# Weight rounding spread evenly over the first batch's first layer, each piece finished one product later, and factors kept in DRAM one by one

## The chip, the core and the metric

The kernel runs on one core of a Trainium2 chip. The metric is device time in microseconds (us) of one execution. A profiled execution gives a trace: start, length and releaser of every instruction on TensorE (PE; its weight loads are PEld), VectorE (DVE), ScalarE (ACT), GpSimd (POOL) and on SyncE (SP), which here only issues DMAs.

## The reference

A q/k-normalised attention followed by a two-layer MLP with the activation h − tanh(h); batch 8, 12 heads, 448 positions, head size 64, model width 768, hidden width 2048. Inputs are float32, but the two weights arrive as float64.

```python
q_n, k_n = (rmsnorm(q, g_q), rmsnorm(k, g_k))
scores = scale * np.matmul(q_n, k_n.transpose(0, 1, 3, 2))
attn = softmax(scores)
x = np.matmul(attn, v).transpose(0, 2, 1, 3).reshape(B * S, H * D)
h = x @ w_in
out = ((h - np.tanh(h)) @ w_out).astype(np.float32)
```

## The kernel before

**Two streams on one TensorE.** Attention is worked off in 48 slots, one for each batch and pair of heads. The first batch's six slots (`first_slot`) run alone, with nothing of the MLP beside them. From then on (`early_slot`, later `slot`) every slot calls `run(gap)` between its parts, and `run` puts matmuls of the MLP of the batch before into the gaps. The order of all instructions on each engine is that in which the program writes them (a manual schedule): an engine that waits holds all that stands behind it.

**The MLP as seven products.** Layer 1 (`hidden`) cuts both matrices into 2x2 blocks and forms the result from 7 products in place of 8, for each of four `SETS` j of hidden rows. `ORDER = (1, 5, 6, 2, 3, 7, 4)` is the order of the products p; a product is 12 matmuls of 128x128 by 224 columns into one PSUM bank out of three ("mm"). I number the first batch's 28 products 0 to 27 in the order in which they run. Products 2, 3 and 7 add onto the banks of 1, 5 and 6, so TensorE may begin them only when VectorE or ScalarE has read the older content (`use`, lines 826 to 860), and each next product 1, 5, 6, 4 takes a bank that an older `use` must have read: L831, L833, L841, L837/L838, L845 and L812 on VectorE release banks.

**Weights of the first batch.** The float64 weights are rounded to float32 on the chip, in 32 pieces (`PIECES`) of 128x768: 0 to 15 of w_in (four for each set), 16 to 31 of w_out. A piece n goes through five stations:

- load: a DMA of 768 KB into a raw buffer (`weight_load`, L272 for w_in in four DMAs, L276 for w_out). From piece 8 on there are three raw buffers (`w_raw`), so the load of piece n+3 waits until piece n is finished (`place_free`).
- a: two instructions on ScalarE (`round_weight_a`, L71 and L72).
- b: three on VectorE (`round_weight_b`, L78, L79, L82).
- c: one on GpSimd (`round_weight_c`, L90), after which the raw buffer is free.
- when a set's four pieces are finished, four sums of them (`combine_weights`; L335 on VectorE, "combos" below, for products 5, 6, 3, 7).

`weight(to)` takes pieces until `to` are taken: for each it issues a of piece n, then b of piece n−1, then c of piece n−1 (`finish_weights`), then the loads that have become possible. So b and c of a piece come when the next piece is taken. The list `due` says how many pieces are to be taken before each of the 28 products; before the change its steps are uneven, so that pieces 7, 8, 9, 10, 11, 12, 13, 14, 15, 16, 17, 18, 19, 20, 21, 22, 23 are taken at products 0, 1, 3, 5, 7, 9, 11, 13, 15, 18, 19, 21, 22, 23, 25, 26, 27.

**Keeping the factors.** The seven factors of each set are written to DRAM (`keep_weights`, L343, seven DMAs of 384 KB in a row on SP) for the later batches. Sets 0 and 3 use one half of the weight memory (`w_half[0]`), set 1 the other, set 2 the ring; a new piece may overwrite a place only when its factor has been kept.

**Layer 2 of the first batch** (`project_first`, L952) uses the rounded w_out directly, 16 matmuls of 448 columns for each of six row blocks, and takes pieces 24 to 31 meanwhile. Later batches (`project`, and `hidden` with b > 0) read the kept factors through a ring of buffers.

**The attention part of a slot** that matters here, in order: totals (L658) and the reciprocal `rs` of them (L663, VectorE, which releases the "sc" bank into which `turn` then transposes at L432); scores of the next slot (L531, two banks at a time) with exp on ScalarE (L537; `p`, then `p_last` for the last keys, then `p_full`); values (L585, L635); division into `xT` (L719). In the `scores` call after the values TensorE takes a bank that `p_last`'s exp must have read.

Of the kernel before, what the change touches and what calls it, by code (L numbers as in the profile page):

```python
# [67 lines left out]
def round_weight_a(nc, raw, dst):  # L68

    lo, hi = raw[:, :, 0], raw[:, :, 1]  # L70
    nc.scalar.activation(dst, hi.bitcast(F32), AF.Abs, scale=2.0**-16)  # L71
    nc.scalar.mul(lo, lo.bitcast(U32), 2.0**-29)  # L72


def round_weight_b(nc, raw, dst):

    bits = dst.bitcast(I32)
    nc.vector.tensor_scalar(out=dst, in0=dst, scalar1=HI_MIN, scalar2=HI_MAX, op0=ALU.max, op1=ALU.min)  # L78
    nc.vector.tensor_scalar(  # L79
        out=bits, in0=bits, scalar1=4, scalar2=1, op0=ALU.logical_shift_left, op1=ALU.logical_shift_right  # L80
    )
    nc.vector.scalar_tensor_tensor(  # L82
        out=bits, in0=raw[:, :, 1], scalar=-(2**31), in1=bits, op0=ALU.bitwise_and, op1=ALU.bitwise_or
    )


def round_weight_c(nc, raw, dst):

    bits = dst.bitcast(I32)
    nc.gpsimd.tensor_tensor(out=bits, in0=bits, in1=raw[:, :, 0], op=ALU.add)  # L90
# [54 lines left out]
def bounded_path(tc, ctx, q, k, v, moe_w_in, moe_w_out, out, g_col, ident, ones, half_ones, neg_half, early):  # L145
# [17 lines left out]
    nc = tc.nc  # L163
# [5 lines left out]
    CD, CF = DM // P, DFF // P  # L169
# [5 lines left out]
    EARLY, PIECES = 8, 2 * CF  # L175
    HS = S // 2
    HC, HF = CD // 2, CF // 2
    SETS = CF // 4
    ORDER = (1, 5, 6, 2, 3, 7, 4)
# [57 lines left out]
    raws = {}  # L237
# [12 lines left out]
    def weight_piece(n):  # L250

        if n < CF:
            j, blk = n // 4, n % 4
            p, low, i = ((1, 0, 0), (0, 1, 0), (4, 1, 1), (2, 0, 1))[blk]
            return 2 * j + low * HF, i, built(j, p)
        i, t = 1 - (n - CF) // HF, n % HF
        if i == 0:
            t = t // 2 + t % 2 * (HF // 2)
        return 2 * t, i, w_half[i][t]

    def weight_load(n):

        f, i, _ = weight_piece(n)
        if n < EARLY:
            raw = stage[:, n % NSTAGE * 2 * DM : (n % NSTAGE + 1) * 2 * DM]
        else:
            raw = wp.tile([P, 2 * DM], I32, name="w_raw", bufs=3)
        if n < CF:
            rows = w_in_words[i * HALF : (i + 1) * HALF, f * 2 * P : (f + 2) * 2 * P]
            rows = rows.rearrange("(c h m r) f -> m h r c f", c=HC, h=2, m=2)  # L270
            for r in range(4):
                nc.sync.dma_start(  # L272
                    out=raw[r * BL : (r + 1) * BL].rearrange("p (c f) -> p c f", c=HC), in_=rows[r // 2, r % 2]
                )
        else:
            nc.sync.dma_start(  # L276
                out=raw.rearrange("p (f c) -> p f c", f=2),
                in_=w_out_words[f * P : (f + 2) * P, 2 * i * HALF : 2 * (i + 1) * HALF].rearrange(
                    "(f p) c -> p f c", p=P
                ),  # L280
            )
        raws[n] = raw.rearrange("p (n w) -> p n w", w=2)

    def weight_dst(n):
        return weight_piece(n)[2].rearrange("p f n -> p (f n)")

    done = [0, 0, 0]
    kept = [0, 0]
    combos = []

    def place_free(n):

        if n < EARLY:
            return n - NSTAGE < done[2]
        return n - 3 < max(done[2], EARLY)

    def load_weights(to):

        while done[0] < min(to, PIECES) and place_free(done[0]):
            weight_load(done[0])  # L300
            done[0] += 1

    def weight(to):

        while done[1] < min(to, PIECES):
            n = done[1]
            round_weight_a(nc, raws[n], weight_dst(n))
            if n:
                round_weight_b(nc, raws[n - 1], weight_dst(n - 1))
            done[1] = n + 1  # L310
            finish_weights(n)
            load_weights(n + (3 if n < EARLY - 3 else 4))
            if kept[1] < kept[0] and n >= 4 * kept[0] + 2:
                keep_weights()
        if done[1] == PIECES > done[2]:
            round_weight_b(nc, raws[PIECES - 1], weight_dst(PIECES - 1))
            finish_weights(PIECES)

    def finish_weights(to):
        while done[2] < to:  # L320
            round_weight_c(nc, raws.pop(done[2]), weight_dst(done[2]))
            done[2] += 1
            if done[2] % 4 == 0 and done[2] <= CF:
                combine_weights(done[2] // 4 - 1)
            keep_w_out(done[2] - 2)
# [13 lines left out]

    def keep_weights():  # L340
        j = kept[1]
        for p in ORDER:
            nc.sync.dma_start(out=w_in_dram[j, p].rearrange("p (f n) -> p f n", f=2), in_=built(j, p))  # L343
        kept[1] = j + 1

    def combine_w_out(f):

# [391 lines left out]
    late = {}  # L739


    due = [EARLY + (m + 1) // 2 for m in range(8)] + [12]
    due += [12 + m // 2 + 1 for m in range(8)]
    due += [CF + HF * (m + 1) // 11 for m in range(11)]
    assert len(due) == 7 * SETS and due[-1] == CF + HF

    def part(name):
# [5 lines left out]
    def products(b, layer, count, width, depth, moving, done_with):  # L753

        took = 4 * HS / ENGINE_NS
        banks = {}  # L760

        def product(j, p, bank, first):
            if b == 0:
                weight(due[7 * j + ORDER.index(p)])
                combine(1)
                while any(c[:2] == (j, p) for c in combos):
                    combine(1)
                w = built(j, p).rearrange("p f (n d) -> p (f n) d", d=P)
            else:
                ring_load(ring_steps.index((b, layer, j, p)) + 5)  # L770
                step_out()
                w = ring_tiles[b, layer, j, p].rearrange("p (n d) -> p n d", d=P)
            for f in range(width):
                for c in range(depth):
                    nc.tensor.matmul(  # L775
                        bank[:, f * HS : (f + 1) * HS], lhsT=w[:, c * width + f, :], rhs=moving[p](c),
                        start=(first and f == 0 and c == 0), stop=(f == width - 1 and c == depth - 1),
                        skip_group_check=not first,
                    )
                    if f < width - 1 or c < depth - 1:  # L780
                        yield took
            now = late["todo"]
            late["todo"] = []
            for fn in now:
                fn()

        for j in range(count):
            use = done_with(j)
            for p in ORDER:
                first = p not in (2, 3, 7)  # L790
                bank = banks[p] = mm_bank() if first else banks[{2: 1, 3: 5, 7: 6}[p]]
                yield from product(j, p, bank, first)
                use(p, bank)
                yield took
# [128 lines left out]
    def project_first(b):  # L923

        g = late["g"]
        for fn in late["todo"]:
            fn()
        late["todo"] = []
        took = 4 * S / ENGINE_NS
        for m in range(CD * CF):  # L930
            k, f = m // CF, m % CF
            n = (k + HC) % CD
            if f == 0:
                bank = mm_bank()
            if f == CF // 2:
                step_out(2)
            if k < HC:
                weight(CF + HF + HF * (m + 1) // (HC * CF))
            elif m < HC * CF + 2:
                keep_w_out(PIECES - 2 + m - HC * CF)  # L940
            elif (m - HC * CF) % 4 == 0 and m - HC * CF <= 4 * HF:
                for fn in late["keep"]:
                    fn()
                late["keep"] = []
                combine_w_out((m - HC * CF) // 4 - 1)
            elif m == CD * CF - 12:
                ring_load(2)
                for fn in late["keep"]:
                    fn()
            elif m == CD * CF - 10:  # L950
                ring_load(4)
            nc.tensor.matmul(  # L952
                bank[:, :S], lhsT=w_out_row(f, n // HC)[:, n % HC * P : (n % HC + 1) * P], rhs=g[:, f, :],
                start=(f == 0), stop=(f == CF - 1),
            )
            if f == CF - 1:
                y = part("s2").rearrange("p f s -> p (f s)")
                nc.scalar.copy(out=y, in_=bank[:, :S])
                store(b, n, y)
            yield took  # L960
        wp_stack.close()
        late["tg"] = pool("tg", bufs=1)
        late["blocks"] = pool("blocks", bufs=1)
# [511 lines left out]
```

## Time and profile before

| | us |
|---|---|
| median of 3 runs (range) | 1382.25 (1381.95 to 1382.39) |
| the profiled execution | 1382.1 |
| its span from first to last instruction | 1380.2 |
| TensorE busy in the span | 1347.5 |
| VectorE busy | 891.1 |
| ScalarE busy | 551.7 |
| GpSimd busy | 553.7 |
| products of the first batch (L775, first matmul to the first of L952) | 79.47 to 184.39 |

Busy shares of the whole span say little about a stretch of some 100 us that lies ahead of 1,100 us of steady work; the stretch has to be read by its own windows and its own timeline. Lengths in the timeline of TensorE are modelled at the end of each group, so the distance from one group's start to the next group's start is the safer measure.

### The profile page before, as it was taken

The numbers are of one execution on the slowest core, as the hardware profiler recorded it, in microseconds if no ns is written. First come the engines' busy times: TensorE is split into PE (matmuls) and PEld (weight loads), VectorE is DVE, ScalarE is ACT, GpSimd is POOL, SyncE is SP. The second block draws the span as 40 slices with busy tenths as digits, with TensorE's granted clock in tenths as the row PEclk, the third lists the DMA queues.
The fourth block names the chain that finished last, engine by engine and source line by source line (L and its number), as shares of the span: only waits on it lengthen the run. The fifth ranks groups of instructions, "written<-read, shape, count | busy, mean of one in ns | idle before, by whom it ended". The sixth has DMA issues, their size and how long they took to land.

```text
span 1380.2 us, 29907 instructions
## 1 busy us (share of the span) xinstructions
PE 1347.5 (98%) x11840; PEld 1127.5 (82%) x11840; DVE 891.1 (65%) x1378; ACT 551.7 (40%) x1314; POOL 553.7 (40%) x345
## 2 busy tenths in 40 slices
PE   7989899999999999999999999999999999999997
PEld 3467654478998998899899889989988998999997
DVE  4999889856854776567765568547765677533311
ACT  7856555244433443334433344334433344211100
POOL 4656566224632356215542346323563155302300
PEclk9999999999999999999999999999999999999999
DMA  7789788965676567567657656765665665556664
GB/s 169 180 226 238 242 255 225 256 166 145 184 199 160 153 189 195 155 145 203 186 147 200 169 147 190 197 156 154 192 190 157 155 196 168 141 162 183 192 187 90
DMA packets 367656, 249.90 MB, mean 181 GB/s; under 512 B 281748, under 2 KB 309780, under 8 KB 367508
## 3 DMA queue, kind: packets, MB, share of 16 engines
q1 hardware_dynamic: 367504, 247.90, 66.7%
q8 instruction: 96, 1.57, 0.5%
q14 instruction: 52, 0.43, 0.1%
q10 hardware_dynamic: 4, 0.00, 0.0%
HBM read 214.40 MB, written 33.42 MB: 180 GB/s over the span
## 4 chain that ended last, share of the span: by engine, by line
PE 89%; DVE 5%; DMA 2%; SPq 2%; ACT 1%; issue 1%; POOL 0%; ACTq 0%; DVEq 0%
PE mm L775 67%; PE sc L531 8%; PE sc L597 6%; PE mm L952 5%; PE sc L585 1%; PE sc L635 1%; DVE w_out L335 1%; DVE rs L663 1%; DMA gT<-in_moe_w_in_dram 1%; DMA w_raw<-in_moe_w_in_dram 1%; DVE w_out L82 1%; SPq L125 1%; DMA w_in<-w_out 1%; DVE xT L719 0%; PE mm L635 0%
## 5 line engine op out<-in xcount | busy, mean ns | idle before, releaser
L775 PE MATMUL mm<-xT,w_f 128*128 128x224 f32 x1392 | 275.6, 354 | 0.0
L775 PEld LDWEIGHTS mm<-xT,w_f 128*128 128x128 f32 x1392 | 262.1, 190 | 10.2 <-issue 10.2
L775 PEld LDWEIGHTS mm<-gT,w_f 128*128 128x128 f32 x1344 | 252.8, 190 | 12.8 <-issue 8.4
L775 PE MATMUL mm<-gT,w_f 128*128 128x224 f32 x1344 | 263.0, 354 | 0.0
L812 POOL TENSOR_TENSOR gT<-s,th 128x448 f32<-128x448 f32 x96 | 119.9, 1256 | 329.2 <-ACT th L811 323.0
L531 PE MATMUL sc<-qT,kT 64*32 64x448 f32 (+1 forms) x3072 | 215.5, 501 | 9.3 <-ACT p_last L537 8.4
L488 POOL TENSOR_TENSOR rr_mine<-rr_mine,neg_half 128x28 f32<-128x28 f32 x33 | 158.1, 4791 | 147.6 <-DVE rr_mine L486 105.4
L775 PE MATMUL mm<-tt,w_f 128*128 128x224 f32 x1044 | 208.6, 353 | 0.0
L775 PEld LDWEIGHTS mm<-tt,w_f 128*128 128x128 f32 x1044 | 197.0, 190 | 4.4 <-issue 4.4
L775 PE MATMUL mm<-tg,w_f 128*128 128x224 f32 x1008 | 197.5, 352 | 0.0
L775 PEld LDWEIGHTS mm<-tg,w_f 128*128 128x128 f32 x1008 | 190.7, 190 | 0.0
L531 PEld LDWEIGHTS sc<-qT,kT 64*32 64x32 f32 x3072 | 70.6, 106 | 78.1 <-issue 55.1
L712 DVE TENSOR_TENSOR xT<-xT,sc 128x448 f32<-128x448 f32 x35 | 21.7, 621 | 138.6 <-PE sc L531 94.9
L597 PE MATMUL sc<-p,v_nat 64*32 64x448 f32 x1120 | 110.5, 536 | 0.0
L734 POOL TENSOR_TENSOR tt<-xT,tt 128x224 f32<-128x224 f32 x23 | 31.2, 1356 | 166.9 <-DVE xT L716 147.2
L537 ACT ACTIVATE p<-sc 128x448 f32<-128x448 f32 x132 | 71.7, 543 | 48.2 <-PE sc L531 36.3
L811 ACT ACTIVATE th<-s 128x448 f32<-128x448 f32 x96 | 54.5, 573 | 69.6 <-DVE s L841 30.2
L687 ACT COPY sum_g<-sum 32x14 f32<-32x14 f32 x280 | 56.3, 201 | 55.4 <-DVE sum L679 44.1
L952 PE MATMUL mm<-gT,w_out 128*128 128x448 f32 x192 | 74.6, 543 | 0.3 <-POOL w_out L90 0.3
L952 PEld LDWEIGHTS mm<-gT,w_out 128*128 128x128 f32 x192 | 35.7, 190 | 37.3 <-issue 34.9
L597 PEld LDWEIGHTS sc<-p,v_nat 64*32 64x32 f32 x1120 | 40.7, 107 | 29.9 <-issue 29.9
L142 POOL TENSOR_TENSOR rr<-rr,neg_half 112x8 f32<-112x8 f32 (+1 forms) x30 | 49.0, 1660 | 34.2 <-DVE rr L141 34.1
(151 smaller groups left out, 1824.0 us busy)
## 6 DMA issues: line engine op xcount, KB each, us to landing
w_f<-w_in SPq DMA_DIRECT2D x196, 384.0 KB, 3.6
w_f<-w_out SPq DMA_DIRECT2D x147, 512.0 KB, 4.5
w_raw<-in_moe_w_out_dram SPq DMA_DIRECT2D x16, 768.0 KB, 5.2
out_dram<-th SPq DMA_DIRECT2D x192, 56.0 KB, 3.6
w_in<-w_out SPq DMA_DIRECT2D x21, 384.0 KB, 5.8
qk_nat<-in_q_dram SPq DMA_DIRECT2D x132, 56.0 KB, 2.2
qk_nat<-in_k_dram SPq DMA_DIRECT2D x132, 56.0 KB, 2.3
v_nat<-in_v_dram SPq DMA_DIRECT2D x72, 96.0 KB, 4.0
```

The costliest lines, as they stand in the source:

```text
L142: nc.gpsimd.tensor_tensor(out=r, in0=r, in1=neg_half[:rows], op=ALU.pow)
L488: nc.gpsimd.tensor_tensor(out=mine, in0=mine, in1=neg_half[:, :1].to_broadcast([P, 2 * NJ]), op=ALU.pow)
L531: nc.tensor.matmul(tiles[h][i * BL : (i + 1) * BL, :n], lhsT=kT[r, c * P + at : c * P + at + BL], rhs=qT[r, first : first + n], start=True ...
L537: nc.scalar.activation(p[:, h, c if c < 2 else 0, :], tiles[h][:, :n], AF.Exp, scale=1.0 if rr is None else rr[:, 0, 2 * c + h : 2 * c + h ...
L597: nc.tensor.matmul(av[g][i * BL : (i + 1) * BL, :S], lhsT=v_nat[keys, h, c, m * BL : (m + 1) * BL], rhs=p[keys, h], start=first, stop=True ...
L687: nc.scalar.copy(out=acc[h * BL : (h + 1) * BL, g], in_=part[g * BL : (g + 1) * BL, h * NJ : (h + 1) * NJ])
L712: nc.vector.tensor_tensor(out=x, in0=x, in1=av[1][:, :S], op=ALU.add)
L734: eng.tensor_tensor(out=t2, in0=x22, in1=t1, op=ALU.subtract)
L775: nc.tensor.matmul(bank[:, f * HS : (f + 1) * HS], lhsT=w[:, c * width + f, :], rhs=moving[p](c), start=(first and f == 0 and c == 0), sto ...
L811: nc.scalar.activation(th, h, AF.Tanh, bias=0.0, scale=1.0)
L812: eng.tensor_tensor(out=g[:, rows, cols], in0=h, in1=th, op=ALU.subtract)
L952: nc.tensor.matmul(bank[:, :S], lhsT=w_out_row(f, n // HC)[:, n % HC * P : (n % HC + 1) * P], rhs=g[:, f, :], start=(f == 0), stop=(f == C ...
```

## The change

Three things. The list `due` takes pieces evenly: eight over the 14 products of sets 0 and 1, eight over the 14 of sets 2 and 3. A new function `settle` does b and c of the pieces already taken; it is called in `weight` behind a of the next piece as before, and also at a product that takes no new piece. And `keep_weights` only lists the factors to be kept: `keep_step` issues them, two behind every piece taken and one at a product without a piece, and all that must be out before a piece overwrites its place.

```diff
         while done[1] < min(to, PIECES):
             n = done[1]
+            keep_step(0, {CF - 4: 0, CF: 1, CF + HF: SETS - 1}.get(n, -1))
             round_weight_a(nc, raws[n], weight_dst(n))
-            if n:
-                round_weight_b(nc, raws[n - 1], weight_dst(n - 1))
+            settle(n)
             done[1] = n + 1
-            finish_weights(n)
             load_weights(n + (3 if n < EARLY - 3 else 4))
             if kept[1] < kept[0] and n >= 4 * kept[0] + 2:
                 keep_weights()
-        if done[1] == PIECES > done[2]:
-            round_weight_b(nc, raws[PIECES - 1], weight_dst(PIECES - 1))
-            finish_weights(PIECES)
+            keep_step(2)
+        if done[1] == PIECES:
+            settle(PIECES)
+
+    def settle(to):
+        for n in range(done[2], to):
+            round_weight_b(nc, raws[n], weight_dst(n))
+            finish_weights(n + 1)
...
     def keep_weights():
         j = kept[1]
-        for p in ORDER:
+        to_keep.extend((j, p) for p in ORDER)
+        kept[1] = j + 1
+
+    to_keep = []
+
+    def keep_step(count, all_of=-1):
+        while to_keep and (count > 0 or to_keep[0][0] <= all_of):
+            j, p = to_keep.pop(0)
             nc.sync.dma_start(out=w_in_dram[j, p].rearrange("p (f n) -> p f n", f=2), in_=built(j, p))
-        kept[1] = j + 1
+            count -= 1
...
-    due = [EARLY + (m + 1) // 2 for m in range(8)] + [12]
-    due += [12 + m // 2 + 1 for m in range(8)]
-    due += [CF + HF * (m + 1) // 11 for m in range(11)]
+    due = [EARLY + (CF - EARLY) * (m + 1) // (7 * SETS // 2) for m in range(7 * SETS // 2)]
+    due += [CF + HF * (m + 1) // (7 * SETS // 2) for m in range(7 * SETS // 2)]
...
             if b == 0:
-                weight(due[7 * j + ORDER.index(p)])
+                to = due[7 * j + ORDER.index(p)]
+                if to > done[1]:
+                    weight(to)
+                else:
+                    settle(done[1])
+                    load_weights(done[1] + 3)
+                    keep_step(1)
...
         late["todo"] = []
+        keep_step(0, SETS - 1)
         took = 4 * S / ENGINE_NS
```

After the change pieces 7 to 23 are taken at products 0, 1, 3, 5, 6, 8, 10, 12, 13, 15, 17, 19, 20, 22, 24, 26, 27, and b and c of a piece come at the product after the one that takes it.

## The prediction

> **What bounds the kernel now.** First the page: TensorE is busy 1347.5 of 1380.2 us, and from about 290 us on the chain of waits is one unbroken run of its matmuls. The first 80 us hold nothing that the change moves. So only the stretch of the first batch's products and what follows it to 200 us can gain or lose, and the windows show it:
>
> ```profile
> span 1380.2 us, 29907 instructions
> PE   7989899999999999999999999999999999999997
> DVE  4999889856854776567765568547765677533311
> ...
> core 0: us, PE busy (x) PEld busy (x) DVE busy (x) ACT busy (x) POOL busy (x), PEclk, DMA share, GB/s
> 80.00:137.00 57.00, 51.99 (x463) 42.92 (x462) 55.25 (x73) 33.50 (x60) 30.08 (x18) 1.00 0.87 234
> 137.00:144.00 7.00, 7.00 (x53) 6.49 (x56) 4.34 (x9) 2.28 (x5) 4.49 (x3) 1.00 1.03 412
> 144.00:172.00 28.00, 22.57 (x221) 16.82 (x214) 23.89 (x28) 16.77 (x33) 15.92 (x9) 0.88 0.68 202
> ```
>
> Two different stretches. Up to 137 us VectorE is full (55.25 of 57 us; its timeline has no idle time before 137.29). From 144 to 172 us TensorE loses 5.4 us, at a granted clock of 0.88, while VectorE has room. Next, TensorE's waits from 84 to 200 us, and the timeline of the longest:
>
> ```profile
> PE sc L531 <- ACT p_last L537: 6.5, 2, 5.4
> PE mm L775 <- DVE s L831: 2.5, 1, 2.5
> PE sc L432 <- DVE rs L663: 1.8, 3, 1.1
> PE mm L952 <- POOL w_out L90: 0.3, 1, 0.3
> ...
> 157.60 2.47 POOL L90 TENSOR_TENSOR w_out<-w_out,w_raw 128x768 int32<-128x768 int32 x1 [1.54 <-PE mm L775]
> 160.09 5.16 SPq L276 DMA_DIRECT2D w_raw<-in_moe_w_out_dram  x2
> 165.73 0.92 ACT L71 ACTIVATE w_out<-w_raw 128x768 f32<-128x768 f32 x1 [6.38 <-DMA w_raw<-in_moe_w_out_dram]
> 167.33 0.76 ACT L537 ACTIVATE p_last<-sc,rr 128x224 f32<-128x224 f32 x2
> 167.80 1.74 PE L531 MATMUL sc<-qT,kT 64*32 64x448 f32 x14 [5.43 <-ACT p_last L537]
> 169.47 2.59 PE L775 MATMUL mm<-tt,w_out 128*128 128x224 f32 x8
> ```
>
> Read it backwards: TensorE waits for `p_last`, which stands behind a of piece 20 on ScalarE, which waits for that piece's DMA, issued only when c of piece 17 had freed the buffer at 160.07. Piece 17 was rounded by a at 147.99; its b was issued when piece 18 was taken, two products later. Piece 20's load had two products (21 to 23) to arrive in.
>
> **What the change removes.** The same attention part, without a wait, takes 4.23 us (start 95.28 to 99.51); here it takes 158.12 to 169.47, 11.35: 7.12 us lost. The eight matmuls behind it take 2.43 us (169.47 to 171.90) against 1.62 (113.62 to 115.24) at the full clock: 0.81. Afterwards b and c of piece 17 come one product after its a, the load of 20 is issued at product 18 and used at 22. Likewise the attention part at 125.68 takes 6.70 to 132.38, 2.47 too long, behind a of piece 14, which waited for its load; its load now follows c of 11, one product after 11 is taken. And 0.40 and 0.25 us at 190 to 197 us (rs late, c of piece 23 late), where VectorE will be ahead. Sum of what can go: 7.12 + 0.81 + 2.47 + 0.65 = 11.05 us.
>
> **What it adds: work ahead of `rs` on a full VectorE.** The number of instructions on the five stations is unchanged; only places move. The order of VectorE's queue before and after is the same up to L831 at 92.89. From there to the reciprocal at 117.79 it held b of pieces 8 to 11 and combos 6, 3, 7 of set 1 and 5 of set 2. Afterwards it holds b of 8 to 12 and combos 6, 3, 7 and 5, 6, 3: one b and two combos more. These rows give the prices:
>
> ```profile
> 99.40 2.07 DVE L335 TENSOR_TENSOR w_out<-w_out,w_out 128x768 f32<-128x768 f32 x1
> 103.06 0.62 DVE L841 TENSOR_TENSOR s<-mm,s 128x448 f32<-128x448 f32 x1
> 103.60 0.55 DVE L78 TENSOR_SCALAR w_f<-w_f 128x768 f32<-128x768 f32 x1
> 117.79 1.55 DVE L663 RECIPROCAL rs<-sc 128x224 f32<-128x224 f32 x1
> 119.39 0.66 PE L432 MATMUL sc<-ident,k_nat 128*128 128x128 f32 x4 [0.21 <-DVE rs L663]
> ```
>
> b is 2.05 us from start to start (103.69 to 105.74 in the chain of waits), a combo 0.87 (92.02 to 92.89) when nothing disturbs it: 2.05 + 2 x 0.87 = 3.79 us. TensorE already waited 0.21 us for that reciprocal, so there is no cover: L432 moves by as much as `rs` does. A combo that meets c on GpSimd took 2.0 (99.40), 1.1 more. One more c (piece 11) falls into the stretch; against it, c of 8 and 9 may fall elsewhere. Bounds: 3.79 − 1.1 = 2.7 and 3.79 + 2 x 1.1 = 6.0; I take 4.5, 3.79 and somewhat over half a collision. Smaller waits on the way are inside this sum, not on top: L841 now stands behind b of 9, so product 7, which began at 104.91 after an L841 that ended at 103.69, will wait 0.8 us or more; L845 stands behind b of 10; L831 for product 11 behind b of 11 and two combos.
>
> [...]
>
> **What replaces the removed waits.** (1) The attention part at 125.68: ScalarE now runs a of 14 and of 15 ahead of `p_last`. The exps of `p` come some 4 us later (they follow the norm's rows on VectorE, pushed by b of 11 and two combos), and a of 15 needs a load that follows c of 12, itself behind the late b. Loads into `w_raw` landed 2.7 to 8.4 us after their issue. Bounds 0 (it lands first) and 2.5 (as before); I take 0.8. (2) Sets 2 and 3: combos of set 3 and b of 16 to 19 come earlier, into the 9.0 us that VectorE idled from 137 to 175 us. Counting its queue from 131 us with the spacings above leaves 0.2 to 2 us between each release and the product that needs it, and `p_last` about 0.6 us late because ScalarE's queue is pushed back. Bounds 0 and 2.5; I take 1.2.
>
> **Edits at nothing.** The 28 keeps are issued one or two at a time, not seven. Each takes SP 0.42 to 1.35 us (L343), as before; what is queued behind them on SP (loads of pieces, v, q and k of slots two to four ahead) comes earlier where seven stood in front, and later where a load that waits for c stands in front: q and k for slot 10 at about 102 rather than 92 us. They are read at 126 us (L130), so 24 us cover it; without that cover a late k would cost TensorE its landing, 3.7 to 4.2 us. Bytes: from 80 to 172 us 57 x 234 + 7 x 412 + 28 x 202 GB/s is 21.9 MB; with two loads more (1.6 MB) in 5 us less it is 270 GB/s, and the window at 137 us moved 412. An overwrite waits for its keep: pieces 12 and 16 follow theirs by at least two products, 5 us, against 4.7 to 7.7 us for a keep to land; product 1's factor, the first overwritten (piece 12), goes out first, some 20 us ahead.
>
> **Sum.** −11.05 + 4.5 + 0.8 + 1.2 = −4.55 us on the profiled execution's 1382.1 us (1380.2 of span and 1.9 around it): 1377.55. The median of the runs is 0.15 above that execution; I predict 1377.6. Own range of this case: best −11.05 + 2.7 = −8.35, 1373.8; worst, with the 0.65 not gained, −10.4 + 6.0 + 2.5 + 2.5 = +0.6, 1382.7.
>
> **Rivals.**
> - *The wait moves but stays* (slower). ScalarE still meets a piece without its data just ahead of `p_last` in the attention part of product 23: piece 20, taken at product 22. For: the order on ScalarE is the same, a of 20 directly ahead of `p_last`. Against: by my count c of 17 ends near 155 us, the DMA lands in 5.2 us (w_out's median), 160, and `p_last` is wanted at 164.5. It decides once c of 17 slips by more than 2.5 us, to where a of 20 (1.7) and an exp (0.4) no longer fit. Then 7.93 is not gained: −4.55 + 7.93 = +3.4, 1385.5. Chance 0.18.
> - *VectorE gives it all back* (no change). b and combos collide with c and GpSimd's L812 at the dear end: 6.0 ahead of `rs`, 2.5 and 2.0 in (1) and (2): −11.05 + 10.5 = −0.55, 1381.5. For: VectorE without idle time until 137 us. Against: collisions are as many as c instructions, and those are not more. Chance 0.17.
> - *The backlog costs little* (faster still): the extra b and combos fall where GpSimd is idle, and collisions go: 2.7 and no new wait, 1373.8. For: GpSimd is busy 30 of 57 us. Chance 0.10.
>
> **How the numbers follow.** The forecast has 0.55. A measurement of this kernel can tell 0.2%, 2.8 us, from no change: faster means below 1379.5, slower above 1385.0. Forecast: most (0.46) below 1379.5, 0.09 same; the third rival below; of the second 0.03 below and 0.14 same; of the slower one, whose loss may be partial, 0.03 same and 0.15 slower. Faster 0.59, same 0.26, slower 0.15. The range 1373.6 to 1384.0 leaves out the upper half and more of the slower rival and a little below.
>
> **What would show it.** Right: the 5.4 us wait for `p_last` gone and no clock below 1.0 from 144 us on; ScalarE not waiting for a load of w_out there; L432's wait for `rs` in the stretch near 120 us grown to 2 to 4 us and product 7 waiting for L841; VectorE without its idle time at 137 us. Layer 2 (first L952 at 184.39) starts 4 to 5 us earlier, and all behind it shifts by that. Wrong: first L952 not earlier than 184, a wait for `p_last` of over 3 us, or the waits near 120 us above 7 us together.

## The result, and the profile after

| | before | after |
|---|---|---|
| median, us (6 runs each) | 1382.01 | 1375.61 |
| range of the runs | 1379.78 to 1382.39 | 1375.15 to 1377.18 |
| profiled execution, its span | 1382.1, 1380.2 | 1375.4, 1373.5 |

The ratio of the runs is 0.9958 with a 95% interval of 0.9945 to 0.9971: by it the change is 5.8 us faster, between 4.0 and 7.6. The forecast was 4.55 us from the profiled execution, or 1377.6 us.

The same windows as before the change, then TensorE's waits from 84 to 200 us (in all, how often, longest):

```profile
80.00:137.00 57.00, 48.34 (x448) 39.62 (x447) 54.90 (x72) 32.10 (x57) 31.74 (x17) 1.00 0.83 234
137.00:144.00 7.00, 7.00 (x39) 7.00 (x38) 6.83 (x8) 3.69 (x5) 4.30 (x2) 1.00 0.96 311
144.00:172.00 28.00, 28.00 (x267) 22.69 (x266) 27.04 (x36) 17.61 (x35) 18.02 (x10) 1.00 0.80 237
...
PE mm L791 <- DVE s L847: 4.0, 2, 2.5
PE sc L443 <- DMA w_in<-w_out: 2.6, 1, 2.6
PE sc L443 <- DVE rs L674: 1.2, 1, 1.2
PE mm L791 <- DVE s L857: 0.8, 1, 0.8
```

The columns of the windows are length, then busy time of TensorE, its weight loads, VectorE, ScalarE and GpSimd, the granted clock, the DMA share and GB/s. From 144 to 172 us TensorE is now busy all the time at clock 1.00 (22.57 of 28 before), and the list of waits has none for `p_last`. From 80 to 137 us it lost 3.65 us of busy time (51.99 to 48.34). VectorE, which had 2.7 us without work from 137 to 144 and 4.1 from 144 to 172, is now busy for 96 to 98% of every one of these windows. L791, L847, L857, L443, L674, L548 are the lines that were L775, L831, L841, L432, L663, L537.

The timeline of the two places that the prediction named: the transposes behind the reciprocal, and the attention part of product 23.

```profile
122.22 1.55 DVE L674 RECIPROCAL rs<-sc 128x224 f32<-128x224 f32 x1
123.83 0.66 PE L443 MATMUL sc<-ident,k_nat 128*128 128x128 f32 x4 [2.61 <-DMA w_in<-w_out]
...
162.17 0.99 ACT L71 ACTIVATE w_out<-w_raw 128x768 f32<-128x768 f32 x1
163.77 1.58 PE L542 MATMUL sc<-qT,kT 64*32 64x448 f32 x16
163.84 0.81 ACT L548 ACTIVATE p_last<-sc,rr 128x224 f32<-128x224 f32 x2
165.28 1.78 PE L791 MATMUL mm<-tt,w_out 128*128 128x224 f32 x8
```

A lesson in reading: the wait of 2.61 us is put down to a DMA of a kept factor. The reciprocal ended at 123.77 and the transpose began at 123.83; e4 below has the same wait of 2.61 us with the reciprocal named. The DMA was only the last event that the profile had seen. At 162.17 a of piece 20 starts with no wait for its load (it waited 6.38 us before the change). `p_last` follows at 163.84 and makes TensorE some 0.6 us late: the part takes 4.83 us, and 4.23 where nothing waits.

The ledger, by starts of groups on TensorE's timeline, sets measured beside forecast (us):

| stretch | before | after | difference | forecast |
|---|---|---|---|---|
| first product to the transposes near 120 us | 39.92 | 45.20 | +5.28 | +4.5 |
| attention part behind product 13 | 6.70 | 4.45 | −2.25 | −1.7 |
| product 14 to the next attention part | 25.74 | 25.89 | +0.15 | } −5.9 |
| attention part in product 23 | 11.35 | 4.83 | −6.52 | } |
| the eight matmuls behind it | 2.43 | 1.62 | −0.81 | −0.8 |
| layer 2's first matmul to the next attention part | 14.20 | 13.07 | −1.13 | −0.65 |

These add up to −5.28, and by batch 1's first product it is −5.17. The spans differ by 6.7: 0.84 more came before the first product, where the instructions of the compute engines stand in the same order in both, and 0.69 in the landing of the last store. Neither was costed; both may be differences between two executions, which one profile of each kernel can't show.

### The profile page after: what moved, and what is told of

Its sections match the earlier page's. It is cut to its first block, busy times and chain, and to the rows that moved or that the text cites. A ratio compares the mean times of both kernels' runs of the same rounds, so it can differ in the third digit from the quotient of the medians.

```text
span 1373.5 us, 29906 instructions
## 1 busy us (share of the span) xinstructions
PE 1344.5 (98%) x11840; PEld 1126.3 (82%) x11840; DVE 888.6 (65%) x1378; ACT 551.1 (40%) x1314; POOL 555.5 (40%) x345
## 4 chain that ended last, share of the span: by engine, by line
PE 93%; DMA 2%; SPq 2%; DVE 1%; ACT 1%; POOL 0%; issue 0%; ACTq 0%; POOLq 0%
PE mm L791 69%; PE sc L542 9%; PE sc L608 6%; PE mm L969 5%; PE sc L646 1%; PE sc L596 1%; DMA w_raw<-in_moe_w_in_dram 1%; PE mm L646 1%; SPq L272 1%; DMA gT<-in_moe_w_in_dram 0%; DMA w_in<-w_out 0%; PE mm L669 0%; PE sc L669 0%; SPq L125 0%; SPq L123 0%
## 5 line engine op out<-in xcount | busy, mean ns | idle before, releaser
L791 PE MATMUL mm<-xT,w_f 128*128 128x224 f32 x1392 | 275.6, 354 | 0.0
L791 PEld LDWEIGHTS mm<-xT,w_f 128*128 128x128 f32 x1392 | 262.1, 190 | 10.2 <-issue 9.5
L791 PEld LDWEIGHTS mm<-gT,w_f 128*128 128x128 f32 x1344 | 252.8, 190 | 12.8 <-issue 8.4
L791 PE MATMUL mm<-gT,w_f 128*128 128x224 f32 x1344 | 263.0, 354 | 0.0
L791 PE MATMUL mm<-tt,w_f 128*128 128x224 f32 x1044 | 208.6, 353 | 0.0
L791 PEld LDWEIGHTS mm<-tt,w_f 128*128 128x128 f32 x1044 | 197.1, 190 | 4.4 <-issue 4.4
L791 PE MATMUL mm<-tg,w_f 128*128 128x224 f32 x1008 | 197.5, 352 | 0.0
L791 PEld LDWEIGHTS mm<-tg,w_f 128*128 128x128 f32 x1008 | 190.7, 190 | 0.0
L548 ACT ACTIVATE p<-sc 128x448 f32<-128x448 f32 x132 | 71.7, 543 | 48.2 <-PE sc L542 36.3
```

Source lines behind the costliest of these rows:

```text
L548: nc.scalar.activation(p[:, h, c if c < 2 else 0, :], tiles[h][:, :n], AF.Exp, scale=1.0 if rr is None else rr[:, 0, 2 * c + h : 2 * c + h ...
L791: nc.tensor.matmul(bank[:, f * HS : (f + 1) * HS], lhsT=w[:, c * width + f, :], rhs=moving[p](c), start=(first and f == 0 and c == 0), sto ...
```

## The experiments

All times below are medians of 5 to 11 runs, with ratios to the kernel before on the same chip. "From the first product" means from the start of the first L791 (L775) group on TensorE; the "first" and "last transposes" are those of the attention parts at products 11 and 20. Line numbers shift by a few from run to run; the names beside the arrow say which instruction it is.

### Which of the three parts does it

The diffs are against the kernel before; e4 is the change without its third part.

```diff
# e1: only the list
+    due = [EARLY + (CF - EARLY) * (m + 1) // (7 * SETS // 2) for m in range(7 * SETS // 2)]
+    due += [CF + HF * (m + 1) // (7 * SETS // 2) for m in range(7 * SETS // 2)]
# e2: only settle, with the old list
+                if to > done[1]:
+                    weight(to)
+                else:
+                    settle(done[1])
+                    load_weights(done[1] + 3)
# e3: only keep_step (two behind a piece, one at a product without)
# e4: the changed kernel, where keep_weights issues all seven
+        keep_step(7)
```

> Only the even list of due pieces; b and c of a piece still come with the next piece, keeps still seven in a row. Theory S (finishing a piece one product later is what lets the loads come early): c of piece 17 comes at product 19, not 18, the wait for p_last in the attention part of product 23 stays at 2 to 5 us, ahead of rs there is only one combo more than before (0.9 us); total 1377 to 1380, slower than the change. Theory D (the even list alone does it, since piece 17 is taken earlier): no wait for p_last above 1 us, total 1373 to 1375, faster than the change because VectorE has less ahead of rs. Theory K (the burst of seven keeps holds SP and the DMA queues): 1380 or more.

> Only b and c one product later, with the old uneven list and keeps seven in a row. Theory S: load of piece 20 is issued one product earlier than before, its wait shrinks from 7.1 us to 1 to 4; one combo more ahead of rs (0.9 us); total 1375 to 1378. Theory D: the wait stays above 5 us because pieces 18, 19 and 20 are still taken at products 21, 22 and 23 in a row; total 1380 to 1382. Theory K: 1380 or more.

> Only the keeps issued one or two at a time; old list, b and c with the next piece. Theories S and D: within 1 us of before, the wait for p_last still 5 to 7 us. Theory K: 2 to 4 us faster than before, since loads no longer stand behind seven keeps on SP.

> The change without its third part: keeps again seven in a row. Theories S and D: within 1 us of the changed kernel (1375.6). Theory K: 2 to 4 us slower than the changed kernel, with loads landing later behind seven keeps and ScalarE waiting for them ahead of p_last.

| run | median us | ratio (95%) | attention part behind product 13 | in product 23 |
|---|---|---|---|---|
| before | | | 6.70 | 11.35 |
| e1 list only | 1379.87 | 0.9987 (0.9978 to 0.9996) | 7.36 | 4.23 |
| e2 settle only | 1378.86 | 0.9977 (0.9968 to 0.9986) | 4.51 | 8.81 |
| e3 keeps only | 1380.18 | 0.9988 (0.9979 to 0.9997) | 4.24 | 10.30 |
| e4 list and settle | 1376.52 | 0.9962 (0.9948 to 0.9975) | 4.24 | 4.24 |
| changed kernel | 1375.61 | 0.9958 (0.9945 to 0.9971) | 4.45 | 4.83 |

Without a wait such a part takes 4.23 us. TensorE's waits for `p_last` in e1 and e2 (timeline of TensorE, with ScalarE's line ahead of it):

```profile
133.07 0.91 ACT L71 ACTIVATE w_out<-w_raw 128x768 f32<-128x768 f32 x1 [2.89 <-DMA w_raw<-in_moe_w_in_dram]
135.61 0.98 PE L531 MATMUL sc<-qT,kT 64*32 64x448 f32 x14 [2.19 <-ACT p_last L537]
```

```profile
162.55 0.90 ACT L71 ACTIVATE w_out<-w_raw 128x768 f32<-128x768 f32 x1 [3.18 <-DMA w_raw<-in_moe_w_out_dram]
164.62 1.74 PE L541 MATMUL sc<-qT,kT 64*32 64x448 f32 x14 [2.88 <-ACT p_last L547]
```

The two parts cure different waits. The list alone (first fence) frees product 23 entirely, against my expectation of 2 to 5 us there, and leaves the wait behind product 13, since piece 15 is then taken at product 13 and its load comes too late. Settle alone (second fence) frees product 13 and leaves 4.6 us in product 23, where pieces 18, 19 and 20 are still taken one after the other. So neither theory S (settle is all) nor D (the list is all) holds; in e4 the two together free both places. That both are needed is not shown: e3, with the keeps alone, freed product 13 too (4.24), and no run has the list and the keeps without settle. Keeping the factors one by one is worth 1.7 us by itself (0.4 to 2.9), mainly behind product 13 (6.70 to 4.24, and 11.35 to 10.30 in product 23). Beside the other two it can't be told from nothing: e4's interval covers the changed kernel's ratio. Theory K falls as a main cause.

### Is the loss ahead of the reciprocal real?

The prediction charged b of piece 12 and two combos ahead of the first reciprocal with 4.5 us; the ledger shows 5.28. If that is a price paid at that place, taking the work away from there must give it back. Diffs against the changed kernel:

```diff
# e5: piece 12 taken a product later, its b behind the reciprocal
+    due[8] -= 1
# e6: the old list for products 0 to 13
+    due[:14] = [EARLY + (m + 1) // 2 for m in range(8)] + [12] + [12 + m // 2 + 1 for m in range(5)]
# e7: no combos at products 7 to 9;  e8: e6 with none at 1, 7, 8, 9
-                combine(1)
+                if 7 * j + ORDER.index(p) not in (7, 8, 9):
+                    combine(1)
```

> The changed kernel with one entry of the due list lowered, so that a of piece 12 comes at product 9 and b at product 10, behind the reciprocal rs. Theory F (VectorE is full up to rs, so what stands ahead of rs is paid one for one by TensorE at the transposes behind it): that transpose comes 2.0 us (b alone) to 3.2 us (b and a collision with c) earlier against the first product, from 45.2 to 42.0 to 43.2; total 1372.5 to 1374. Rival W (the reciprocal waits for TensorE or a DMA, as the releaser named in the changed kernel's profile says): under 0.7 us earlier, total within 1 us of 1375.6.

> The changed kernel with the old due list for products 0 to 13 and the new one behind. Theory F: ahead of rs only one combo more than in the kernel before, the transpose at 40.5 to 42.5 us from the first product against 39.9 before and 45.2 in the changed kernel; waits for p_last under 1.5 us; total 1372 to 1374.5. Theory D of the first runs (the evenness of the list matters for the loads): the later pieces 14 and 15 bring back a wait for p_last of 2 us or more, total 1375 or above.

> The changed kernel with no combos at products 7, 8 and 9, so that set 2's four combos come at products 10 to 13, behind rs. Theory F: the transpose comes 2.6 us (three combos) or up to 3.7 earlier, at 41.5 to 42.6 us from the first product; combos pile up behind rs instead, so up to 1 us of it is lost again at products 12 and 13; total 1372.5 to 1374. Rival W: within 1 us of 1375.6.

> Old list for products 0 to 13, new behind, and no combos at products 1, 7, 8 and 9. Theory F: nothing ahead of rs that the kernel before did not have, and the wait of product 4 for L831 (2.5 us in all kernels so far) shrinks by one combo, to 1.6; the transpose at 39 to 40.5 us; total 1370 to 1373, the fastest. Rival W: as the run with the old first half.

| run | median us | ratio (95%) | first transposes | last transposes | layer 2, all from the first product |
|---|---|---|---|---|---|
| before | | | 39.92 | 72.42 | 104.92 |
| changed | 1375.61 | 0.9958 (0.9945 to 0.9971) | 45.20 | 75.53 | 100.75 |
| e5 | 1376.95 | 0.9973 (0.9963 to 0.9983) | 43.29 | 78.45 | 103.02 |
| e6 | 1375.43 | 0.9965 (0.9951 to 0.9979) | 42.43 | 76.02 | 100.65 |
| e7 | 1376.55 | 0.9969 (0.9957 to 0.9981) | 42.45 | 76.52 | 101.72 |
| e8 | 1375.93 | 0.9963 (0.9950 to 0.9977) | 40.59 | 75.59 | 100.66 |

The first transposes moved about as theory F said, by 1.9 to 4.6 us; rival W (a DMA) is out. But nothing of it arrived: the last transposes came at 75.5 to 78.5 us, and no run was clearly faster than the changed kernel. The windows from the first product to the last transposes in the changed kernel, and in e8, each with the last transposes and, for the changed kernel, the reciprocal ahead of them:

```profile
78.63:154.16 75.53, 66.86 (x596) 55.70 (x588) 73.01 (x97) 40.84 (x77) 43.56 (x24) 1.00 0.83 245
152.56 1.55 DVE L674 RECIPROCAL rs<-sc 128x224 f32<-128x224 f32 x1
154.16 0.66 PE L443 MATMUL sc<-ident,k_nat 128*128 128x128 f32 x4
```

```profile
79.08:154.67 75.59, 67.47 (x589) 55.57 (x589) 73.98 (x97) 41.88 (x77) 43.90 (x24) 1.00 0.81 239
154.67 0.65 PE L443 MATMUL sc<-ident,k_nat 128*128 128x128 f32 x4 [1.86 <-DMA w_in<-w_f]
```

VectorE runs 97 instructions in both and is busy 73.0 of 75.5 us and 74.0 of 75.6. In e8 TensorE waits 1.86 us at the last transposes (again put down to a DMA, where the reciprocal ended 0.06 us ahead), and the changed kernel didn't wait there: what is taken away ahead of the first reciprocal is met again at the last. In e6, e7 and e8 the last reciprocal ends 76.0, 76.5 and 75.5 us from the first product, in the changed kernel 75.5, and each time TensorE follows within 0.06 us. e5 is another matter. Its last reciprocal ends at 75.7 as well, but TensorE comes 2.79 us later: a wait of 1.49 us for `p_last` behind product 13 came back (an attention part of 6.82), and the twelve matmuls behind it took 3.86 us, not 2.37, at a lowered clock (0.85 granted from 128.27 to 138.27 us; they began at 135.73).

In the kernel before, VectorE was not the limit at this place:

```profile
145.87 1.55 DVE L663 RECIPROCAL rs<-sc 128x224 f32<-128x224 f32 x1
151.89 0.60 PE L432 MATMUL sc<-ident,k_nat 128*128 128x128 f32 x4
```

The reciprocal ended 67.95 us from the first product, 4.47 us ahead of the transposes. Two b and three combos more now stand ahead of it, and it ends 7.53 us later. The theory that I formed from this (V): in the changed kernel VectorE is the bound over the whole stretch, so the time at its end is the sum of its work, and the order inside moves only the places where TensorE waits.

### Is VectorE the bound?

```diff
# e9: b and c of pieces 0 to 6 in the slot that takes them
             weight(s + 2)
+            settle(done[1])
         combine(2)
# e10, e11: L82 (idempotent) twice for pieces 8 to 11, or for 19 to 22
             round_weight_b(nc, raws[n], weight_dst(n))
+            if 8 <= n < 12:
+                bits = weight_dst(n).bitcast(I32)
+                nc.vector.scalar_tensor_tensor(
+                    out=bits, in0=raws[n][:, :, 1], scalar=-(2**31), in1=bits, op0=ALU.bitwise_and, op1=ALU.bitwise_or
+                )
# e12: e9 with the old list for products 0 to 13, as e6
```

> The changed kernel with settle called also at the end of each of the first batch's own slots, so that b and c of pieces 0 to 6 come a slot earlier and one b less is left for the products. Theory V (VectorE is full from the first product to the reciprocal behind product 20, so the time there is the sum of its work, wherever that stands): the last reciprocal's transpose comes 2 us earlier against the first product, from 75.5 to 73.5, layer 2 from 100.7 to 98.7, the wait of product 4 shrinks from 2.5 to about 0.5 us; total 1373 to 1374.5. Rival L (what stands ahead of the single waits decides): the wait of product 4 shrinks, and the rest shifts by the same 2 us; it differs from V only in the runs with doubled work. Rival B (the earlier slots are full too, b and combos that move into them delay them by as much): layer 2 earlier against the first product, but the first product later by as much, total within 1 us of 1375.6.

> The changed kernel with the last step of b (L82, 0.96 us on VectorE, the same result when done twice) done twice for pieces 8 to 11: 3.9 us more of VectorE work ahead of the first reciprocal. Theory V: layer 2 starts 3.5 to 5 us later against the first product (104.2 to 105.7), total 1379 to 1381. Rival O (the early waits are made up later, as the three runs with less work there suggest): under 1.5 us later.

> The same doubling for pieces 19 to 22, whose b stands behind the reciprocal of product 20: 3.9 us more of VectorE work after the last place where TensorE waits for it. Theory V: layer 2 within 1 us of the changed kernel's 100.75, total 1375 to 1377, unless VectorE has no slack there either. Rival Q (VectorE is the bound up to layer 2): 3 to 5 us later, total 1379 or more.

> The run with settle in the first batch's own slots, with the old due list for products 0 to 13. Theory V: VectorE was busy 68.4 of 70.8 us there from the first product to the transpose behind product 20, so moving b and combos from ahead of the first reciprocal to behind it gains nothing at the last one: that transpose again at 70 to 71.5 us from the first product, the wait near 40 us smaller and one near 71 us in its place; total 1371.5 to 1373.5. Rival L (each wait counts by itself): the waits of 1.55 and 2.61 near 36 and 40 us go and nothing comes for them, the transpose at 67 to 69 us, total 1369 to 1371.

| run | median us | ratio (95%) | first transposes | last transposes | layer 2 |
|---|---|---|---|---|---|
| e4 (for e10, e11) | 1376.52 | 0.9962 (0.9948 to 0.9975) | 45.48 | 77.19 | 101.76 |
| e10 twice, pieces 8 to 11 | 1380.50 | 0.9992 (0.9984 to 1.0001) | 49.49 | 81.06 | 105.63 |
| e11 twice, pieces 19 to 22 | 1377.06 | 0.9967 (0.9954 to 0.9980) | 45.49 | 77.20 | 102.46 |
| e9 settle in slots | 1372.55 | 0.9937 (0.9924 to 0.9950) | 40.41 | 70.78 | 96.00 |
| e12 e9 and old first half | 1372.09 | 0.9934 (0.9921 to 0.9948) | 36.91 | 70.52 | 95.15 |

e10 and e11 are compared with e4, whose execution, like theirs, ran the matmuls behind product 4's wait at a lowered clock (in all three 0.76, from 15 to 22 us behind the start of the first product; last section). Four times 0.98 is 3.9 us of VectorE work. Ahead of the first reciprocal it costs 3.87 us at the last transposes and 3.87 at layer 2 (105.63 − 101.76): one for one, nothing is made up. Behind the last reciprocal it costs 0.70 (102.46 − 101.76): there VectorE has slack. Rivals O and Q fall, and V gave both numbers. One limit: in e4 and e10 the last reciprocal ended 1.32 and 1.26 us ahead of the transposes, so TensorE was the later of the two there, and most of the loss stood at the first transposes already (45.48 to 49.49). e10 alone would also fit a price paid at the first reciprocal and carried along; against that stand e6 to e8, which gained at the first and had nothing left of it at the last. No run doubled work between the two.

e9 puts VectorE work into time that it had free: before the products, where b of pieces 0 to 6 waited for the next slot. The windows from the first product to the last transposes, and the waits of TensorE from 78 to 200 us, in e9:

```profile
79.51:150.29 70.78, 66.57 (x597) 55.78 (x589) 68.40 (x90) 40.87 (x77) 41.04 (x22) 1.00 0.89 262
...
PE sc L443 <- DMA w_in<-w_out: 2.6, 1, 2.6
PE mm L791 <- DVE s L847: 1.5, 1, 1.5
```

Seven VectorE instructions and 4.61 us of its work fewer lie in the stretch, and it is 4.75 us shorter. I had expected 2 us (one b of three instructions); the other four instructions left because VectorE came to the first product with less of the slot before still undone. The first product itself started at 79.51 against 78.63; how much of that is the price of the fuller slots and how much the execution can't be told from one profile each. By the ratios e9 is faster than the changed kernel, and its interval of 0.9924 to 0.9950 reaches the other's (0.9945 to 0.9971) only at its end. e12 tested V once more, with work moved from ahead of the first reciprocal to behind it: the waits near 36 and 40 us shrink, and one of 1.85 us at the last transposes comes in their place. Its two largest waits of TensorE:

```profile
PE sc L443 <- DVE rs L674: 2.4, 2, 1.9
PE mm L792 <- DVE s L848: 0.9, 2, 0.6
```

Last transposes 70.52 against 70.78, as V said, and not the 67 to 69 of its rival. In time e12 can't be told from e9. Both beat the kernel before by some 9 us.

## Why the prediction was right, point by point

- **What bounds the kernel.** The long wait for `p_last` was a wait for piece 20's load, and it went: 6.52 of 7.12 us, with the 0.81 us of the lower clock in full (0.65 granted from 169.47 to 171.90 us before the change, 1.00 after it). e1 and e2 show that the step named too few causes for its end. "b and c of piece 17 come one product after its a" was given as the reason; e1, which lacks just that, freed product 23 as well, because the even list takes piece 17 two products earlier. Settle's own share lies at product 13 and in making the list bearable there.
- **The wait behind product 13** (2.47 to go, 0.8 to come): −2.25 measured, so 0.2 came.
- **Work ahead of `rs`**: 3.79 us of work by the rows plus half a collision gave 4.5; 5.28 measured, as much as 3.79 and 1.4 collisions of 1.1 us. The bounds of 2.7 to 6.0 held. The waits named on the way were there: product 7 for L857 (0.82 us), product 11 for L847 (1.49), both inside the sum as said.
- **The step that was mis-sized in kind**: "L432 moves by as much as `rs` does", charged to what stands ahead of the first reciprocal. The amount was right and the place was not the cause: e5 to e8 took 1.9 to 4.6 us away at that place and gained nothing at the end. What costs is the whole of VectorE's work up to the last reciprocal. Read that way the change pays 3.11 us there (72.42 to 75.53): VectorE's busy time rises by 5.26 (67.75 to 73.01), its idle time falls by 2.15. That the sum came out with 4.5 at the first place is luck in part: e8 paid 0.67 there (40.59 against 39.92) and came to the last transposes at 75.59 all the same. The prediction counted the queue only up to 131 us by the loss, and from there by "0.2 to 2 us between each release and the product that needs it". It saw small margins where it should have seen a full engine.
- **Sets 2 and 3** (1.2 to come): 0.15 and, in the attention part, 0.60. The 0.6 us by which `p_last` would be late was right.
- **Layer 2** (−0.65): −1.13. The two waits of 0.40 and 0.25 went. The other 0.48 seems to belong to the same two stops, where the weight loads had waited 1.12 and 0.97 us; the prediction counted only the matmuls' idle time.
- **Rivals.** "The wait moves but stays" did not happen in the changed kernel, but e1 and e5 are that rival at product 13. "VectorE gives it all back" was right about VectorE being the limit and wrong about the sum. The edits costed at nothing cost nothing; the keeps alone even gained 1.7 us, which the prediction hadn't seen.
- **The total**, 5.28 us by the ledger against 4.55, is off by the −0.5 in layer 2's start and −1.0 in the two replaced waits, against +0.8 ahead of `rs`.

## What to carry to other kernels

When a stretch is short of one engine and TensorE's waits in it name that engine at several places, sum that engine's busy time over the whole stretch before costing a single wait. Where it came to 97%, as here, taking work from ahead of one wait only moved the wait to the next place. Doubling an instruction is a cheap test (3.9 us in, 3.87 us out), and it needs the other test, work taken away, beside it. What helps is work moved out of the stretch, into time when the engine idles, ahead of it (e9) or, as e11 suggests, behind the last place that waits. And a load that is late is cured at the step that frees its buffer; look which other piece then becomes the late one.

## What the runs showed of the hardware

The wait of product 4 for L847 is 2.53 or 2.54 us in eleven of the profiles, but what follows isn't the same. In the profiles of before, after and e5 the granted clock stayed at 1.00 there; in eight others it fell, to a mean of 0.76 to 0.80 from 15 to 22 us behind the start of the first product; in e1 so (windows just behind the wait):

```profile
92.00:95.00 3.00, 2.09 (x7) 1.98 (x8) 3.00 (x4) 0.00 (x0) 2.00 (x1) 0.76 1.07 235
95.00:99.00 4.00, 4.00 (x74) 2.03 (x77) 3.93 (x7) 0.79 (x2) 1.45 (x1) 0.75 0.02 3
```

From the matmuls behind the wait to the first product behind the attention part it is 5.95 us in the three and 7.50 to 7.57 in the eight: the lower clock cost 1.55 to 1.62 us each time. What decides it is open. In the eight, TensorE had also waited 0.20 to 1.19 us for a reciprocal just ahead of the first product, in the three it hadn't. The lower clock may be one reason why single executions of one kernel differ by 2 to 3 us, which one profile of each can't show, and it is why e10 and e11 were read against e4. In e9 and e12, where the wait is gone, and in e8, where it is 1.67 us, the clock stayed at 1.00 there.
